# State product of an attention stage in four quadrants of TensorE, with one decay table left in PSUM and one shared bank for transposes and gate products

## The chip, the cores and the metric

The kernel runs on one core of one Trainium2 chip. Its time is the device time of one execution in microseconds (us). Six queues work side by side: PE (TensorE's matmuls; PEld is its loading of weights), DVE (VectorE), ACT (ScalarE), POOL (GpSimd), SP (SyncE, which here only issues DMAs) and the DMA engines themselves. Each engine takes its instructions in the order in which the program gives them to it, and waits for semaphores of the others.

## The reference, cut to what matters

Three stages follow one another: a recurrent attention, a mixture of 8 experts with one expert for each token, and a dense layer.

```python
for t in range(S):                       # attention, B=4, H=8, S=768, D=48
    cur = einsum('bhd,bhe->bhde', u * k[t], v[t])
    y[t] = einsum('bhd,bhde->bhe', r[t], state + cur)
    state = w[..., None] * state + einsum('bhd,bhe->bhde', k[t], v[t])
x = y as (3072, 384)
out[token] = gate * (relu(x @ w1[e]) @ w2[e])      # e = argmax of x @ w_gate
h = out @ w_in; result = (h - tanh(h)) @ w_out
```

Only the way in which the attention stage is laid out on the engines changes; all that is computed stays.

## The kernel before, in words

The attention stage is written out as a sequence of 24 blocks of 128 tokens: six chunks `c` of the sequence, and for each the four batch entries `b`; block `n` is `(c, b) = divmod(n, 4)`. The order of the work is the order in which the code of the main loop (L756 to L834) calls its helpers; no planner stands behind it. In each turn `n` of the loop the engines get:

- SP: the two loads of block n+3 (`fetch`, L239 and L240), and the store of a finished block (`xout_g`, L582), which waits for ACT. Five sets of buffers are in use.
- POOL: `side` (L342, L348) and `side_kh` (L357), products of r, k, u and a decay table for block n+2, and in `state_add` the decay of the old state (L407).
- DVE: `diag_sum` (L362), `scale` (L333: r and k of block n+1 times their decay tables), `mask` (L383: two predicated copies that put the scores under the diagonal into `am`), `state_add` (L408), and, once in four blocks, the steps of the gate (`gate`, `rank_of`, `rank_in`).
- PE: `outp` of block n-1, `state_mm` (L396) and `scores` (L378) of block n, a transpose of a finished block (`xout_t`, L573) and, once in four blocks, the gate's products (`logits` L455, `logits2` L464, `rank_mm`, `idx_mm`).
- ACT: the copies of `outp`'s results (L439), `state_copy` (L421), `xout_g` (L580), eight diagonal blocks of `am` for block n+1 (`diag`, L369), and steps of the gate.

Heads go in pairs: head h = 2j + q, and the 48 rows of q = 0 and q = 1 stand in partitions 16 to 63 and 64 to 111. `outp` adds two products in PSUM. The first (L429, from block 4 on) multiplies the state with r: its weights `Sb` are a block-diagonal copy of the state `Sc`, 112 by 128 for each pair j, so that one matmul does both heads of a pair. The second (L434) multiplies v with `am`, 128 rows by 48 columns of weights, left or right half of the array by q. The zeros of `Sb` are written once at the start (`zero_states`, L322). Every f32 matmul stands in the trace as two records. The two decay tables are made in PSUM (`PRKp`), used there for the first four blocks, and then copied to SBUF by ACT (`scale_rows`, L337).

In between, the loop prepares weights of the first expert: `w_load` (L76) loads them, and `w_split` rounds them on ACT (L84) and takes the rest on DVE (L85); the table `SPLITS` (L753) says after which block. A step of `w_split` on DVE waits for its step on ACT.

Of the kernel before, what the change touches and what calls it, by code (L numbers as in the profile page):

```python
# [15 lines left out]
ALU = mybir.AluOpType  # L16
# [14 lines left out]
def rwkv_moe_moe_kernel(ctx: ExitStack, tc: tile.TileContext, rk_t, rkv, pk, u, wp1, wp2, out):  # L31
# [168 lines left out]
    pkg = ap_.tile([P, E * HP], F32, name="pkg")  # L200
# [5 lines left out]
    Sc = [ap_.tile([PT, HP, D], F32, name=f"Sc{b}") for b in range(B)]  # L206
    Sb = [ap_.tile([PT, HP, P], F32, name=f"Sb{b}") for b in range(B)]
# [3 lines left out]
    PRK = ap_.tile([PT, 2, HP, P], F32, name="PRK")  # L211
# [36 lines left out]
    def gate_rows():  # L248
        nc.vector.memset(pkg, 0.0)
        for q in range(2):  # L250
            nc.sync.dma_start(out=pkg[64 * q:64 * q + D], in_=pk[q][:, 2 * HP:])
# [9 lines left out]
    def gate_cols():  # L261
        nc.gpsimd.memset(wgp, 0.0)
        nc.gpsimd.tensor_copy(out=wgp[:, :, 0:E], in_=pkg.rearrange("p (j e) -> p j e", e=E))
# [56 lines left out]
    def zero_states():  # L320
        for b in range(B):
            nc.scalar.mul(out=Sb[b], in_=ident[0:PT].unsqueeze(1).to_broadcast([PT, HP, P]), mul=0.0)  # L322
# [12 lines left out]
    def scale_rows():  # L335
        for k in range(2):
            nc.scalar.copy(out=PRK[:, k], in_=PRKp[k])  # L337
# [61 lines left out]
    def state_add(n):  # L399
# [3 lines left out]
        if c == 0:  # L403
            nc.vector.tensor_copy(out=Sc[b], in_=Pp[0:PT])
        else:
            sw = at2.tile([PT, HP, D], F32, tag="sw", name="sw")
            nc.gpsimd.tensor_tensor(out=sw, in0=Sc[b], in1=bc(pq[:, :, 8:9], [PT, HP, D]), op=ALU.mult)  # L407
            nc.vector.tensor_tensor(out=Sc[b], in0=sw, in1=Pp[0:PT], op=ALU.add)  # L408
        st["S", b] = n
# [1101 lines left out]
```

## Time and profile before

| | |
|---|---|
| median of 3 runs | 778.57 us (778.37 to 778.96) |
| the profiled execution, its own time | 778.02 us |
| its span, first to last instruction | 776.3 us |
| PE, PEld, DVE busy in the span | 98%, 90%, 83% |
| ACT, POOL busy in the span | 67%, 57% |
| granted clock of TensorE, mean | 0.999 |

The busy shares are averages over three stages with different limits. The attention stage fills about the first 125 us; after it PE is busy nearly all the time. Times in a timeline are counted from the start of the span. A matmul's record includes its way through the array, so records of one engine overlap, and what a group of matmuls costs is read from the start of its first record to the start of the next group. A record's own duration on DVE or ACT is likewise a little longer than the distance to the next one.

### The profile page before, as it was taken

The numbers are of one execution on the slowest core, as the hardware profiler recorded it, in microseconds if no ns is written. First come the engines' busy times: TensorE is split into PE (matmuls) and PEld (weight loads), VectorE is DVE, ScalarE is ACT, GpSimd is POOL, SyncE is SP. The second block draws the span as 40 slices with busy tenths as digits, with TensorE's granted clock in tenths as the row PEclk, the third lists the DMA queues.
The fourth block names the chain that finished last, engine by engine and source line by source line (L and its number), as shares of the span: only waits on it lengthen the run. The fifth ranks groups of instructions, "written<-read, shape, count | busy, mean of one in ns | idle before, by whom it ended". The sixth has DMA issues, their size and how long they took to land.

```text
span 776.3 us, 14324 instructions
## 1 busy us (share of the span) xinstructions
PE 762.8 (98%) x5040; PEld 695.4 (90%) x5040; DVE 645.8 (83%) x1135; ACT 523.3 (67%) x1136; POOL 440.9 (57%) x434
## 2 busy tenths in 40 slices
PE   8899999999999999999999999999999999999997
PEld 7788878998999999999889899899899899898887
DVE  7999898698898998975798888888888888888893
ACT  7999987463544554555787766776776677677881
POOL 7999972385867777766265353534435344343533
PEclk9999999999999999999999999999999999999999
DMA  8988954366899799973100010000001000000100
GB/s 253 273 258 262 288 178 145 124 192 188 245 240 297 202 291 290 251 228 104 48 1 1 1 41 1 1 21 21 1 1 41 0 1 22 21 1 0 42 1 41
DMA packets 34559, 89.63 MB, mean 115 GB/s; under 512 B 5403, under 2 KB 12608, under 8 KB 34482
## 3 DMA queue, kind: packets, MB, share of 16 engines
q1 hardware_dynamic: 30288, 78.67, 33.9%
q0 software_dynamic: 4192, 9.99, 4.2%
q8 instruction: 41, 0.67, 0.4%
q14 instruction: 36, 0.29, 0.1%
q10 hardware_dynamic: 2, 0.00, 0.0%
HBM read 72.90 MB, written 15.74 MB: 114 GB/s over the span
## 4 chain that ended last, share of the span: by engine, by line
PE 51%; issue 2%; ACT 1%; POOL 1%; POOLq 0%
PE h L1345 25%; PE o L1393 23%; PE y L1118 1%; PE hps L1093 1%; POOL out_dram L1406 0%; PE o L1345 0%; POOL g L1382 0%; POOLq L1452 0%; POOL xb L1382 0%; ACT mk L1355 0%; ACT s L1353 0%; POOLq L1506 0%; ACT xb L1381 0%; ACT z L1349 0%; ACT t L1351 0%
## 5 line engine op out<-in xcount | busy, mean ns | idle before, releaser
L1382 POOL TENSOR_TENSOR g<-t,g 128x512 fp32r<-128x512 f32 x93 | 120.4, 1295 | 176.8 <-ACT g L1381 126.7
L1345 PE MATMUL h<-xb,ring 128*128 128x512 f32 x855 | 213.6, 395 | 0.0
L1393 PE MATMUL o<-ring,g 128*128 128x384 f32 x1116 | 209.3, 336 | 0.0
L1393 PEld LDWEIGHTS o<-ring,g 128*128 128x128 f32 x1116 | 196.1, 188 | 8.2
L1345 PEld LDWEIGHTS h<-xb,ring 128*128 128x128 f32 x855 | 159.7, 188 | 30.4
L85 POOL TENSOR_TENSOR ring<-stg,ring 128x384 fp32r<-128x384 f32 x102 | 106.0, 1061 | 55.3 <-ACT ring L84 42.9
L1349 ACT ACTIVATE z<-h 128x512 f32<-128x512 f32 x95 | 56.8, 597 | 95.3 <-PE h L1345 95.3
L1118 PE MATMUL y<-h,ring 128*128 128x256 f32 (+7 forms) x576 | 114.1, 342 | 0.6 <-DVE h L1097 0.6
L1093 PE MATMUL hps<-xt,ring 128*128 128x472 f32 (+6 forms) x504 | 105.6, 353 | 0.1
L1118 PEld LDWEIGHTS y<-h,ring 128*128 128x128 f32 x576 | 101.3, 188 | 4.1 <-DVE h L1097 1.0
L1361 DVE TENSOR_TENSOR t<-t,h 128x512 f32<-128x512 f32 x95 | 65.2, 686 | 40.1 <-ACT t L1351 39.7
L1093 PEld LDWEIGHTS hps<-xt,ring 128*128 128x128 f32 x504 | 90.6, 188 | 3.7 <-DVEq L1232 0.4
L1366 DVE COPY_PREDICATED t<-mk,h 128x512 f32<-128x512 uint32 x95 | 71.5, 752 | 10.1 <-DVE h L1364 0.5
L1096 ACT ACTIVATE h<-hps 128x256 fp32r<-128x256 f32 (+7 forms) x64 | 32.0, 500 | 64.6 <-PE hps L1093 64.1
L84 ACT CAST ring<-stg 128x384 fp32r<-128x384 f32 x152 | 70.1, 513 | 7.9 <-DMA stg<-in_wp_dram 4.1
L1363 DVE SCALAR_TENSOR_TENSOR h<-s,h 128x512 f32<-128x512 f32 x95 | 66.2, 696 | 10.6 <-ACT g L1381 0.9
L1353 ACT ACTIVATE s<-z,gb 128x512 f32<-128x512 f32 x96 | 69.7, 726 | 0.0
L1355 ACT ACTIVATE mk<-z,gt 128x512 f32<-128x512 f32 x96 | 69.3, 722 | 0.0
L1364 DVE SCALAR_TENSOR_TENSOR h<-z,h 128x512 f32<-128x512 f32 x95 | 66.1, 695 | 3.3
L1362 DVE TENSOR_TENSOR h<-h,z 128x512 f32<-128x512 f32 x95 | 65.9, 693 | 0.0
L1381 ACT CAST g<-t 128x512 fp32r<-128x512 f32 x93 | 57.6, 619 | 9.7 <-DVE t L1366 7.8
L369 ACT ACTIVATE am<-ident,dt 128x128 f32<-128x128 f32 x192 | 58.6, 390 | 1.9 <-DVE dt L362 1.7
(255 smaller groups left out, 1092.3 us busy)
## 6 DMA issues: line engine op xcount, KB each, us to landing
stg<-in_wp_dram SPq DMA_DIRECT2D x64, 384.0 KB, 4.7
n<-in_rkv_dram SPq DMA_DIRECT2D x24, 576.0 KB, 5.0
d<-in_wp_dram SPq DMA_DIRECT2D x32, 384.0 KB, 5.8
t<-in_rk_t_dram SPq DMA_DIRECT2D x24, 384.0 KB, 6.9
wdec<-dcf SPq DMA_DIRECT2D x32, 192.0 KB, 5.3
xd<-xs SPq DMA_DIRECT2D x24, 192.0 KB, 2.5
stg<-wdec SPq DMA_DIRECT2D x12, 384.0 KB, 4.6
wl<-wdec SPq DMA_DIRECT2D x2, 768.0 KB, 6.2
```

Source lines behind the costliest of these rows:

```text
L84: nc.scalar.copy(out=dst[:, 0, sl], in_=of)
L85: eng.tensor_tensor(out=dst[:, 1, sl], in0=of, in1=dst[:, 0, sl].bitcast(F32), op=ALU.subtract)
L1093: nc.tensor.matmul(ps, lhsT=wf(a, kk), rhs=xt[e][b][:, kk, :], start=(n == 0), stop=(n == 8))
L1118: nc.tensor.matmul(yps[d], lhsT=wf(a)[:, d * P:(d + 1) * P], rhs=h2[:, b, :], start=(f == 0 and n == 0), stop=(f == CH1 - 1 and n == 2))
L1345: nc.tensor.matmul(ps, lhsT=wf(a, kk), rhs=xb[j][:, b, kk, :], start=(n == 0), stop=(n == 8))
L1353: nc.scalar.activation(out=s, in_=z, func=ACTF.Square, scale=G_K ** 0.5, bias=gb)
L1355: nc.scalar.activation(out=mk, in_=z, func=ACTF.Relu, scale=-1.0, bias=gt2)
L1363: nc.vector.scalar_tensor_tensor(out=ps, in0=s, scalar=G_K * G_D, in1=ps, op0=ALU.add, op1=ALU.mult)
L1364: nc.vector.scalar_tensor_tensor(out=ps, in0=z, scalar=G_A, in1=ps, op0=ALU.subtract, op1=ALU.mult)
L1366: nc.vector.copy_predicated(out=t, mask=mk.bitcast(U32), data=ps)
L1382: nc.gpsimd.tensor_tensor(out=g[:, 1, :], in0=ww, in1=g[:, 0, :].bitcast(F32), op=ALU.subtract)
L1393: nc.tensor.matmul(ops[q], lhsT=gg[i][:, b, q * P:(q + 1) * P], rhs=wf(a), start=(f == 0 and n == 0), stop=(f == CH2 - 1 and n == 2))
```

## The change

Block products are laid out anew. The state has two buffers that alternate by chunk (`Sc[0]`, `Sc[1]`), and no block-diagonal copy is made: `zero_states` and `state_copy` go. The state's product is eight matmuls instead of four, each with 64 or 48 rows and 48 columns of weights, at row half q and column half g of the array; head h = 2(2i + g) + q now lands at partitions 64g of bank `Yp[q]`. The products with `am` go in the order of q. Gate weights, the copies of `Yp` and the stores follow the new order of heads. The table for r stays in PSUM, in a bank of its own (`K`), so `scale` is two instructions of 512 elements in every block, and only the other table is copied. One bank (`X`) serves the transposes and the gate's first product; only from block 23 on they take turns with `K`. In the turns with `logits` the transpose stands behind `state_mm` instead of ahead of `outp`. `SPLITS` moves its first four steps one block ahead.

The core of the diff:

```diff
-    Sc = [ap_.tile([PT, HP, D], F32, name=f"Sc{b}") for b in range(B)]
-    Sb = [ap_.tile([PT, HP, P], F32, name=f"Sb{b}") for b in range(B)]
+    Sc = [[ap_.tile([PT, HP, D], F32, name=f"Sc{k}{b}") for b in range(B)] for k in range(2)]
...
-        if n < B:
-            for k in range(2):
-                nc.vector.tensor_tensor(out=t[:, k], in0=t[:, k], in1=PRKp[k], op=ALU.mult)
-        else:
-            nc.vector.tensor_tensor(out=t, in0=t, in1=PRK, op=ALU.mult)
+        for k, by in enumerate((PRKp[0], PRKp[1] if n < B else PRK1)):
+            nc.vector.tensor_tensor(out=t[:, k], in0=t[:, k], in1=by, op=ALU.mult)
...
-    def state_copy(n):
-        c, b = seq[n]
-        if c == C - 1:
-            return
-        for q in range(2):
-            rows = slice(64, PT) if q else slice(0, 64)
-            nc.scalar.copy(out=Sb[b][rows, :, 64 * q:64 * q + D], in_=Sc[b][rows, :, :])
...
         if c > 0:
+            for i in range(2):
+                for g in range(2):
+                    for q in range(2):
+                        rows = slice(64, PT) if q else slice(0, 64)
+                        j, p0 = 2 * i + g, 64 * g
+                        nc.tensor.matmul(Yp[q][p0:p0 + D, i, :], lhsT=Sc[c % 2][b][rows, j, :],
+                                         rhs=t_b[n % NB][rows, 0, j, :], start=(i == 0), stop=False)
+        for q in range(2):
             for j in range(HP):
-                nc.tensor.matmul(Yp[j % 2][:, j // 2, :], lhsT=Sb[b][:, j, :], rhs=t_b[n % NB][0:PT, 0, j, :],
-                                 start=(j < 2), stop=False)
-        for j in range(HP):
-            for q in range(2):
-                p0 = 64 * q
-                nc.tensor.matmul(Yp[j % 2][p0:p0 + D, j // 2, :], lhsT=n_b[n % NB][:, 2, 2 * j + q, :],
-                                 rhs=am[:, q, j, :], start=(c == 0 and j < 2), stop=(j >= 2))
+                i, p0 = j // 2, 64 * (j % 2)
+                nc.tensor.matmul(Yp[q][p0:p0 + D, i, :], lhsT=n_b[n % NB][:, 2, 2 * j + q, :],
+                                 rhs=am[:, q, j, :], start=(c == 0 and i == 0), stop=(i == 1))
...
+        turns.append(name)
+        tag = "K" if "both" in st and len(turns) % 2 else "X"
+        return ps1.tile([P, HP, P], F32, tag=tag, name=name)
...
-        SPLITS = {9: (0, 0), 13: (0, 1), 17: (0, 2), 19: (0, 3), **{NN - 3 + k: (1, k) for k in range(3)}}
+        SPLITS = {8: (0, 0), 12: (0, 1), 16: (0, 2), 18: (0, 3), **{NN - 3 + k: (1, k) for k in range(3)}}
...
-            if xs_of:
+            with_logits = n % B == 1 and n > B
+            if n == NN - 1:
+                st["both"] = True
+            if xs_of and not with_logits:
                 xout_t(xs_of[0])
```

On PE, where the state's product meets the product with `am` (here in block 10), before; yh_161 and yh_162 are the two banks `Yp`, and the first two rows stand there twice in a row:

```order
L429 MATMUL yh_161<-t_125,Sb_149 128x128
L429 MATMUL yh_162<-t_125,Sb_149 128x128
L434 MATMUL yh_161<-am,n_130 48x128 x2
L434 MATMUL yh_162<-am,n_130 48x128 x2
L434 MATMUL yh_161<-am,n_130 48x128 x2
L434 MATMUL yh_162<-am,n_130 48x128 x2
L396 MATMUL yh_163<-n_131,kh_160 64x48
```

On PE at the same place, now; the first two rows stand there four times in a row:

```order
L418 MATMUL yh_161<-t_125,Sc_145 48x128
L418 MATMUL yh_162<-t_125,Sc_145 48x128
L423 MATMUL yh_161<-am,n_130 48x128 x4
L423 MATMUL yh_162<-am,n_130 48x128 x4
L390 MATMUL yh_163<-n_131,kh_160 64x48
```

The state's matmuls are twice as many and narrower, and the four products of q = 0, which need the first masked half of `am` alone, stand ahead of the four of q = 1.

On DVE, around a step of `w_split` (L85, one of the first four) and the scaling that follows, before:

```order
L408 TENSOR_TENSOR Sc_144<-sw,yh_163 112x192
L561 TENSOR_TENSOR idf<-idf,sm 128x32
L85 TENSOR_TENSOR ring_69<-stg,ring_69 128x384
L362 TENSOR_REDUCE dt<-rku 128x8
L333 TENSOR_TENSOR t_125<-t_125,PRK 112x1024
L383 COPY_PREDICATED am<-mlt,A_1373 128x512
```

On DVE around the same step, now:

```order
L402 TENSOR_TENSOR Sc_143<-sw,yh_163 112x192
L525 SCALAR_TENSOR_TENSOR sm<-sm,RK 128x4
L527 TENSOR_TENSOR ohh<-sm,q_79 128x16
L530 TENSOR_TENSOR ol<-iotaf,sm 128x512
L85 TENSOR_TENSOR ring_69<-stg,ring_69 128x384
L356 TENSOR_REDUCE dt<-rku 128x8
L328 TENSOR_TENSOR t_129<-t_129,prkK 112x512
L328 TENSOR_TENSOR t_129<-t_129,PRK_154 112x512
L377 COPY_PREDICATED am<-mlt,A_1315 128x512
```

The step stands behind `rank_in` (three rows of the gate) one block earlier, and the one product of 1024 elements with a table in SBUF has become two of 512, of which the first reads its table (prkK) from PSUM.

On ACT, from the copies of `Yp` to the rounding of the same step (L84), before:

```order
L439 COPY y<-yh_161 128x2x128
L439 COPY y<-yh_162 128x2x128
L549 ACTIVATE rh<-hv,pid 128x4x32
L421 COPY Sb_147<-Sc_143 64x4x48
L421 COPY Sb_147<-Sc_143 48x4x48
L580 ACTIVATE xs<-Xps,gt 128x384
L369 ACTIVATE am<-ident,dt 128x128 x8
L84 CAST ring_69<-stg 128x384
```

On ACT at the same step, now:

```order
L428 COPY y<-yh_161 128x2x128
L428 COPY y<-yh_162 128x2x128
L577 ACTIVATE xs<-Xps,gt 128x384
L363 ACTIVATE am<-ident,dt 128x128 x8
L84 CAST ring_69<-stg 128x384
```

The two copies of the state are gone from every block, and the gate's row (L549) is not in this one.

## Rows read from the trace of the kernel before

**Rows 1.** Busy time by stretch: us, then each engine's busy time (instructions); later stages
```profile
core 0: us, PE busy (x) PEld busy (x) DVE busy (x) ACT busy (x) POOL busy (x), PEclk, DMA share, GB/s
130.00:365.00 235.00, 233.79 (x1388) 223.34 (x1387) 196.61 (x375) 118.45 (x267) 158.22 (x155) 1.00 0.76 220
365.00:776.00 411.00, 406.59 (x2047) 367.22 (x2045) 332.02 (x488) 290.92 (x526) 176.54 (x146) 1.00 0.04 16
```

**Rows 2.** The same view, cycles of four blocks in the attention stage
```profile
46.68:66.15 19.47, 19.17 (x280) 16.73 (x278) 18.04 (x39) 17.80 (x57) 18.86 (x20) 1.00 0.84 262
66.15:86.04 19.89, 19.44 (x280) 16.73 (x279) 18.86 (x40) 18.01 (x57) 18.49 (x19) 1.00 0.91 282
86.04:105.84 19.80, 18.76 (x265) 16.19 (x263) 17.57 (x39) 18.02 (x57) 18.33 (x18) 1.00 0.79 251
```

**Rows 3.** Waits from 20 to 106 us: us in total, times, longest us
```profile
PE yh L434 <- DVE am L383: 3.4, 7, 0.9
DVE ring L85 <- ACT ring L84: 3.3, 3, 1.4
PEld Xps L573 <- ACT xs L580: 2.5, 3, 0.8
```

**Rows 4.** Timeline of DVE: start us, us, engine line op [idle before <-releaser]
```profile
56.07 0.92 DVE L85 TENSOR_TENSOR ring<-stg,ring 128x384 fp32r<-128x384 f32 x1 [1.15 <-ACT ring L84]
...
62.26 1.22 DVE L333 TENSOR_TENSOR t<-t,PRK 112x1024 f32<-112x1024 f32 x1
63.39 1.34 DVE L383 COPY_PREDICATED am<-mlt,A 128x512 f32<-128x512 uint32 x2
```

**Rows 5.** Timeline of ACT ahead of the step of w_split in block 9
```profile
51.16 0.65 ACT L439 COPY y<-yh 128x256 f32<-128x256 f32 x2 [0.39 <-PE yh L434]
...
51.99 0.70 ACT L421 COPY Sb<-Sc 64x192 f32<-64x192 f32 x2
52.72 0.58 ACT L580 ACTIVATE xs<-Xps,gt 128x384 f32<-128x384 f32 x1
...
55.53 0.50 ACT L84 CAST ring<-stg 128x384 fp32r<-128x384 f32 x1
```

**Rows 6.** Groups by line, 20 to 106 us: count | busy us, mean ns
```profile
L85 DVE TENSOR_TENSOR ring<-stg,ring 128x384 fp32r<-128x384 f32 x3 | 3.8, 1282 | 3.3 <-ACT ring L84 3.3
```

**Rows 7.** Timeline of DVE behind the attention's loads
```profile
107.31 0.55 DVE L85 TENSOR_TENSOR ring<-stg,ring 128x384 fp32r<-128x384 f32 x1
```

**Rows 8.** Groups by line, first 230 us
```profile
L333 DVE TENSOR_TENSOR t<-t,PRK 112x1024 f32<-112x1024 f32 x20 | 32.9, 1646 | 0.0
```

**Rows 9.** Instructions of tile t on DVE: duration ns min/median/max, first and last start
```profile
L333 DVE TENSOR_TENSOR t<-t,PRK x18: 1208/1554/2496, 23.7 to 108.2; 112x1024 f32<-112x1024 f32 x18
L331 DVE TENSOR_TENSOR t<-t,prk x4: 678/680/682, 14.6 to 20.8; 112x512 f32<-112x512 f32 x4
```

**Rows 10.** Timeline of DVE and POOL at one long product of scale
```profile
32.25 2.46 DVE L333 TENSOR_TENSOR t<-t,PRK 112x1024 f32<-112x1024 f32 x1
...
32.62 1.00 POOL L342 TENSOR_TENSOR rk<-n 128x384 f32<-128x384 f32 x1
...
33.70 1.87 POOL L348 TENSOR_TENSOR rku<-rk,ub 128x384 f32<-128x384 f32 x1
```

**Rows 11.** Timeline of PE, blocks 11 and 12
```profile
63.55 1.06 PE L429 MATMUL yh<-t,Sb 112*128 112x128 f32 x8
64.53 1.22 PE L434 MATMUL yh<-am,n 128*48 128x128 f32 x15
...
66.15 1.16 PE L378 MATMUL A<-t 64*128 64x128 f32 x16
67.24 1.07 PE L455 MATMUL lps<-y,wgp 128*32 128x512 f32 x8
...
69.72 1.08 PE L434 MATMUL yh<-am,n 128*48 128x128 f32 x16
70.63 0.61 PE L396 MATMUL yh<-n,kh 128*64 128x48 f32 x16
71.17 0.60 PE L378 MATMUL A<-t 64*128 64x128 f32 x5
```

**Rows 12.** Timeline of PE in block 2
```profile
22.67 1.48 PE L434 MATMUL yh<-am,n 128*48 128x128 f32 x15 [0.92 <-DVE am L383]
23.89 0.32 PE L396 MATMUL yh<-n,kh 128*64 128x48 f32 x3
```

More of the change, by code (lines that the diff above doesn't have):

```diff
@@ L262, in gate_cols @@
         nc.gpsimd.memset(wgp, 0.0)
-        nc.gpsimd.tensor_copy(out=wgp[:, :, 0:E], in_=pkg.rearrange("p (j e) -> p j e", e=E))
+        for g in range(2):
+            rows = slice(64 * g, 64 * g + 64)
+            nc.gpsimd.tensor_copy(out=wgp[rows, :, 0:E].rearrange("p (q i) e -> p q i e", q=2),
+                                  in_=pkg[rows].rearrange("p q (i g e) -> p g q i e", g=2, e=E)[:, g])
     def in_range():
@@ L328, in scale @@
         t = t_b[n % NB][0:PT]
-        if n < B:
-            for k in range(2):
-                nc.vector.tensor_tensor(out=t[:, k], in0=t[:, k], in1=PRKp[k], op=ALU.mult)
-        else:
-            nc.vector.tensor_tensor(out=t, in0=t, in1=PRK, op=ALU.mult)
+        for k, by in enumerate((PRKp[0], PRKp[1] if n < B else PRK1)):
+            nc.vector.tensor_tensor(out=t[:, k], in0=t[:, k], in1=by, op=ALU.mult)
     def scale_rows():
-        for k in range(2):
-            nc.scalar.copy(out=PRK[:, k], in_=PRKp[k])
+        nc.scalar.copy(out=PRK1, in_=PRKp[1])
     def side_rk(n):
@@ L568, in xout_t @@
         if bank is None:
-            ps = ps1.tile([P, HP, P], F32, tag="X", name="Xps", bufs=2)
+            ps = x_bank("Xps")
         else:
@@ L672, in by_token @@
                     rT, kT = t_s[0:PT, 0], t_s[0:PT, 1]
-                    yc = ps1.tile([P, HP, P], F32, tag="X", name="yc", bufs=2)[:, 0, 0:HP]
-                    nc.vector.memset(yc, 0.0)
+                    yc = [x_bank("yc")[:, 0, 0:2] for q in range(2)]
+                    for q in range(2):
+                        nc.vector.memset(yc[q], 0.0)
                     with tc.For_i(0, P, 1) as t:
                         nc.vector.tensor_copy(out=oh, in_=bc(ident[:, bass.ds(t, 1)], [P, 64]))
-                        vb = ps1.tile([P, HP, P], F32, tag="X", name="vb", bufs=2)[:, :, 0:D]
+                        vb = sm[:, 300:300 + HP * D].rearrange("p (j d) -> p j d", d=D)
                         for q in range(2):
@@ L687, in by_token @@
                             for j in range(HP):
-                                p0, p1 = 64 * q, PT if q else 64
-                                nc.tensor.matmul(yc[p0:p0 + D, j:j + 1], lhsT=cur[p0:p1, j, :],
+                                p0, p1, o = 64 * q, PT if q else 64, 64 * (j % 2)
+                                nc.tensor.matmul(yc[q][o:o + D, j // 2:j // 2 + 1], lhsT=cur[p0:p1, j, :],
                                                  rhs=one2[p0:p1, :], start=True, stop=True)
-                        nc.vector.tensor_copy(out=st["y", c][:, :, b, bass.ds(t, 1)], in_=yc.unsqueeze(2))
-                        nc.vector.tensor_tensor(out=Sc[b], in0=Sc[b], in1=bc(wcol.unsqueeze(2), [PT, HP, D]), op=ALU.mult)
-                        nc.vector.tensor_add(out=Sc[b], in0=Sc[b], in1=kv)
+                        for q in range(2):
+                            nc.vector.tensor_copy(out=st["y", c][:, 2 * q:2 * q + 2, b, bass.ds(t, 1)], in_=yc[q].unsqueeze(2))
+                        nc.vector.tensor_tensor(out=Sc[0][b], in0=Sc[0][b], in1=bc(wcol.unsqueeze(2), [PT, HP, D]), op=ALU.mult)
+                        nc.vector.tensor_add(out=Sc[0][b], in0=Sc[0][b], in1=kv)
                 logits(c)
@@ L775, in rwkv_moe_moe_kernel @@
                 at_step(n, 6, rank_row)
-                if n > 1:
-                    state_copy(n - 1)
-            for k, m in enumerate(xs_of):
-                if k:
-                    xout_t(m)
-                xout_g(m)
+            if n > 1 and n < NN:
+                state_mm(n)
+            if xs_of and with_logits:
+                xout_t(xs_of[0])
+            if xs_of:
+                xout_g(xs_of[0])
             if 0 < n < NN - 1:
@@ L784, in rwkv_moe_moe_kernel @@
             if n < NN:
-                if n > 1:
-                    state_mm(n)
                 scores(n)
+                for m in xs_of[1:]:
+                    xout_t(m)
+                    xout_g(m)
                 mask(n)
```

40 lines of the change are left out of this document (18 added, 22 removed).

## The prediction

> **What bounds the kernel now.** I read the busy times by stretch first. From 130 us to the end PE is busy 233.8 of 235 and 406.6 of 411 us at a granted clock of 1.00, its 2.4 GHz level [rows 1]: nothing there is touched, and whatever the attention stage ends earlier, the end comes earlier too. So the question is the attention stage alone, and there I took cycles of four blocks, since the gate's steps return every fourth block. Three of them last 19.47, 19.89 and 19.80 us, and in each of them PE is busy 18.8 to 19.4, DVE 17.6 to 18.9, ACT 17.8 to 18.0 and POOL 18.3 to 18.9 us [rows 2]. Four engines are nearly full at once; to take work from one alone helps only as far as the next one.
>
> Which of them leads? A record of PE includes its way through the array, so PE looks busy through short waits: the product with `am` takes 0.91 us from its start to the next group when nothing holds it (69.72 to 70.63), and 1.22 us in block 2, where its first record has waited 0.92 us for the mask of DVE and the later ones wait for the mask's second half [rows 11, 12]. Altogether PE's named waits for that mask are 3.4 us [rows 3]. DVE's records do not overlap like that. In the three cycles it is idle 1.43, 1.03 and 2.23 us, 4.7 together, and 3.3 of these are three waits of `w_split` for ACT [rows 2, 3]. Without them DVE is full. So DVE leads, PE follows closely, and ACT enters by these three waits.
>
> **The change part by part.** The sum is made against the profiled execution, 778.02 us (span 776.3 and 1.7 around it), which lies 0.55 under the median of 778.57.
>
> *Waits of DVE for ACT.* In block 9 ACT needs 55.53 - 51.16 = 4.37 us from the copies of `Yp` to the rounding step; the two copies of the state are 52.72 - 51.99 = 0.73 of it, and a row of the gate lies in the 0.83 ahead of them [rows 5]; DVE stood 1.15 us before the step [rows 4]. Now the state's copies are gone from every block (which takes 4 x 0.73 = 2.9 us per cycle from ACT, of 17.8 to 18.0), the gate's row is not in the block to which the step has moved, and DVE has three rows of the gate ahead of it. ACT comes over 0.73 us earlier, DVE later, and ACT has 2.9 us more slack in a cycle, so I take all three waits as gone: **-3.3 us** (bounds 0 and -3.3).
>
> *The steps themselves.* Those three steps took 1282 ns on average [rows 6], one later on 0.55 us [rows 7]. The excess, 3 x 0.73 = 2.2 us, comes from POOL, as with the scaling below. Where they will meet POOL now nobody can read from this trace; I take half, **-1.1 us** (0 to -2.2).
>
> *The scaling.* Twenty products of 1024 elements take 1646 ns on average [rows 8]; to the next instruction it is about 0.09 less (62.26 to 63.39 is 1.13 for a record of 1.22 [rows 4]), so 1.56. Undisturbed it is 1.13; the mean disturbance is 0.43. The half whose table is in PSUM took 678 to 682 ns in the first blocks, hardly varying, while POOL worked [rows 9], so 0.59 to the next one; the SBUF half undisturbed is 0.57. That makes 1.16, and the question is how much of the 0.43 is left. The row to go by is the product at 32.25: it takes 2.46 us, and it ends 1.09 us after POOL's product that ran from 32.62 to 33.62, which is its own undisturbed time; POOL's next product, at 33.70, then takes 1.87 instead of 1.00 [rows 10]. That looks like one waiting for the other to finish, not like two sharing. If so, an instruction of half the length waits as long as a whole one, and each block has 1.16 + 0.43 = 1.59 against 1.56: 20 x 0.03 = **+0.6 us**. Bounds: never disturbed, 20 x -0.40 = -8.0; always as at 32.25 (1.24 more than undisturbed), 20 x (1.16 + 1.24 - 1.56) = +17. I take the mean wait, because POOL's work per cycle stays the same.
>
> The Trainium skill ("SBUF — State Buffer", section "Who interferes with whom") says the same as that row: a VectorE instruction with two inputs in SBUF and a GpSimd instruction that reads SBUF exclude each other for a whole instruction, and one with a single SBUF input is left alone. By this rule the sum is the one above; by shared bandwidth it would be 20 x (1.16 + 0.22 - 1.56) = -3.6 us, 4.2 us lower, which is one of the rivals.
>
> *The state's product on PE.* Today 8 records take 64.53 - 63.55 = 0.98 us, 0.123 each, one after another [rows 11]. It becomes 16 records, four for each quarter of the array. No row shows four quarters at work. What rows show [rows 11] is two row halves side by side (`scores`: 16 records in 67.24 - 66.15 = 1.09, 0.068 each), two column halves (16 in 0.91, 0.057 each), and four column strips: `logits`, whose 8 records of 512 elements would be 8 x 4 x 0.123 = 3.9 us one after another, is over in 1.07. Four strips ran in parallel there, so I take four quarters too: 16 x 0.123 / 4 = 0.49. The way in which the array is divided changes once more per block; `scores`, at whose borders it changes, takes 0.18 more than the 16 records of the column halves, and I take that as the price: 0.67 in all, 0.31 less per block. From PE's 18.8 to 19.4 us per cycle this leaves 17.5 to 18.2. Bounds: pairs only, 0.91 to 1.09 and 0.18, 0.1 to 0.3 more per block; no overlap, 16 x 0.123 + 0.18 = 2.15, 1.17 more. As DVE leads, a gain on PE is worth **0** by itself; what it buys is that PE does not stop the 4 us that DVE gives up.
>
> The Trainium skill ("TensorEngine Tiling (Array Packing)", section "Tiling Modes") has a rule against the change: to switch the tiling mode drains TensorE. It names no time; the 0.18 above agrees with it. Without such a price the product would cost 0.49 and the sum would stay as it is, since PE is not first.
>
> *The order of the second product.* It can start on the first masked half. In a block like block 2, where PE waits for the mask, the second half is then all that is left, and the 1.22 - 0.91 = 0.31 us go [rows 12]. Two early blocks look like this, with DVE idle for part of the block: 2 x 0.31 = **-0.6 us**. Later blocks are DVE's, and have nothing from it.
>
> *Edits I cost at nothing.* The zeroing of `Sb` and one table copy leave ACT in the first blocks, where PE's warming matmuls and the mask come last. The gate's weights take a second small copy on POOL. SP's stores wait for ACT, which hands them over 0.73 us earlier, so the loads behind them go out earlier; the first cycle moved 262 x 19.47 = 5.1 MB, and the same in 18.4 us is 277 GB/s, under the 282 of the second cycle [rows 2]. The single bank: a transpose now waits for ACT to have read the one before. ACT is done with that 0.65 + 0.58 = 1.23 us after the end of `outp`, and PE comes back to it after `state_mm` and `scores`, 0.54 + 1.09 = 1.63 us [rows 5, 11]. That leaves 0.4 us of cover; if it goes, each of some 17 transposes costs up to 0.58 us.
>
> Sum: -3.3 - 1.1 + 0.6 - 0.6 = **-4.4 us**. Against the profiled run that is 773.6, against the median 774.2; I say **774.0 us**.
>
> **The rivals.**
> 1. *DVE's disturbance shrinks* with the length of its SBUF product, or the new phase misses POOL. For it: the fastest product takes 1208 ns and half of them under 1554 [rows 9], so many meet nothing today. Against: the row at 32.25. Shared bandwidth gives 774.0 - 4.2 = 769.8, and more than half of the lower bound about 768.
> 2. *PE takes the lead back*, because the quarters overlap only in pairs or because the single bank's cover fails. Pairs put PE at 19.2 to 20 us per cycle, the bank at up to 4 x 0.58 = 2.3 over 17.5 to 18.2: both as long as today. What is left are the first blocks and little else: about 777.5.
> 3. *Slower: the quarters do not overlap at all.* Then PE needs 18.8 to 19.4 plus 4 x 1.17 = 4.7, at least 23.5 us per cycle against 19.7; in five cycles 5 x 3.8 = 19: 797. The point from which it decides is a product of about 1.3 us, where PE passes today's cycle. Against it: every division of the array that the trace shows does overlap.
> 4. *The scaling meets POOL more often*, because it now asks for SBUF at another moment. From 0.22 us more per block (4.4 over 20) the gain is gone: 778.5; from 0.3 more it is slower by what can be measured.
>
> **How the numbers follow.** The forecast 0.52, rival 1 0.20, rival 2 0.12, rival 3 0.06, rival 4 0.10. What a measurement of this kernel can tell from no change is about 0.2%, 1.6 us. The forecast's own range is 771 to 777, from its bounds other than the scaling's. The range reaches down to rival 1 (768.0) and up through rivals 2 and 4 to 778.5; it leaves out rival 3, the worse part of rival 4 and what lies beyond rival 1, together under 0.2. Faster by over 0.2% (under 777.0) are nearly all of the forecast and rival 1, and a part of 2: 0.75. Within 0.2%: the rest of 2 and half of 4: 0.15. Slower: 3 and part of 4: 0.10.
>
> **What would show it.** In the profile of the changed kernel: no wait of `w_split` on DVE for ACT in the attention stage; the PSUM half of the scaling near 0.68 us, the SBUF half between 0.66 and 1.9; the 16 records of the state's product in 0.5 to 0.7 us from start to start; cycles of four blocks near 18.5 us; DVE idle under 1 us per cycle; the transposes' wait for ACT not above today's 2.5 us. I am wrong if the state's product takes over 1 us, if the SBUF half is near its own time throughout (then the gain is larger), or if the later stages, PE's alone until now, do not start earlier by what the attention stage saves.

## The result, and the profile after

The changed kernel is faster: 771.68 us (median of 4 executions, 771.04 to 772.78) against 778.77 us beside it, a ratio of 0.9909 with a 95% interval of 0.9894 to 0.9925. Predicted were 774.0 us, with 768.0 to 778.5 as the range. Two later sets, each beside its own runs of the kernel before, gave 774.58 and 773.90 us, ratios 0.9946 (0.9928 to 0.9964) and 0.9944 (0.9920 to 0.9968). So the gain is 4 to 7 us, and its size varies from set to set; the experiments and the last section say what is known of why.

The profiled execution (772.78 us, span 771.1) answers to [rows 2] and [rows 1] as follows. Busy time by stretch: us, then each engine's busy time (instructions), granted clock, DMA share, GB/s; the first three rows are the cycles of blocks 8 to 19:

```profile
47.41:64.89 17.48, 17.48 (x312) 14.25 (x310) 17.20 (x43) 15.54 (x50) 16.09 (x18) 1.00 0.96 294
64.89:82.61 17.72, 17.57 (x312) 14.26 (x311) 17.45 (x43) 15.54 (x50) 16.31 (x18) 1.00 0.98 302
82.61:101.03 18.42, 17.38 (x297) 13.70 (x296) 18.18 (x42) 15.63 (x49) 16.27 (x18) 1.00 0.98 304
...
130.00:365.00 235.00, 233.81 (x1350) 223.40 (x1349) 191.41 (x363) 117.15 (x264) 159.30 (x155) 1.00 0.78 222
365.00:771.00 406.00, 401.33 (x2016) 361.98 (x2015) 331.42 (x487) 288.79 (x521) 174.34 (x143) 1.00 0.03 13
```

The twelve blocks took 59.16 us and take 53.62 in this trace, so 5.54 less. DVE is now idle 0.28, 0.27 and 0.24 us per cycle, where it was idle 1.43, 1.03 and 2.23 [rows 2]. The later stages are PE's as before, and carry what the attention stage saves to the end.

Groups of DVE (count | busy us, mean ns of one | idle before), the first two over the first 230 us, the third from 20 to 106 us, to be set beside [rows 6, 8]:

```profile
L328 DVE TENSOR_TENSOR t<-t,PRK 112x512 f32<-112x512 f32 x20 | 20.3, 1015 | 0.0
L328 DVE TENSOR_TENSOR t<-t,prkK 112x512 f32<-112x512 f32 x24 | 16.2, 677 | 0.0
...
L85 DVE TENSOR_TENSOR ring<-stg,ring 128x384 fp32r<-128x384 f32 x4 | 2.5, 616 | 0.0
```

The steps of `w_split` wait for nothing now (3.3 us before) and take 616 ns instead of 1282. Four of them stand in the twelve blocks now and three before, where the fourth follows at 107.31 us [rows 7]. So that is 3.3 + 3 x 1.28 - 4 x 0.62 = 4.7 of the 5.54 us. The scaling takes 0.59 + (1.015 - 0.09) = 1.52 us to the next instruction, where it took 1.56. The other two traces of the changed kernel have 985 and 958 ns for the half in SBUF, so 1.49 and 1.46 us.

The timeline of PE between blocks 11 and 12, beside [rows 11]:

```profile
62.27 0.64 PE L570 MATMUL Xps<-ident,y 128*128 128x128 f32 x4
62.84 0.66 PE L418 MATMUL yh<-t,Sc 64*48 64x128 f32 x16
63.42 1.10 PE L423 MATMUL yh<-am,n 128*48 128x128 f32 x16
64.35 0.61 PE L390 MATMUL yh<-n,kh 128*64 128x48 f32 x16
```

The state's product takes 63.42 - 62.84 = 0.58 us for 16 records, 0.98 before for 8. Four quarters of the array do work side by side.

### The profile page after: what moved, and what is told of

It reads as the page before. It is cut to its first block, busy times and chain, and to the rows that moved or that the text cites. A ratio compares the mean times of both kernels' runs of the same rounds, so it can differ in the third digit from the quotient of the medians.

```text
span 771.1 us, 14624 instructions
## 1 busy us (share of the span) xinstructions
PE 755.7 (98%) x5200; PEld 684.6 (89%) x5200; DVE 639.2 (83%) x1155; ACT 509.1 (66%) x1091; POOL 430.9 (56%) x435
## 4 chain that ended last, share of the span: by engine, by line
PE 51%; issue 2%; ACT 1%; POOL 1%; POOLq 0%
PE h L1346 25%; PE o L1394 24%; PE y L1119 1%; PE hps L1094 1%; POOL out_dram L1407 0%; PE o L1346 0%; POOL g L1383 0%; POOLq L1453 0%; POOL xb L1383 0%; ACT s L1354 0%; ACT mk L1356 0%; POOLq L1507 0%; ACT xb L1382 0%; ACT z L1350 0%; ACT t L1352 0%
## 5 line engine op out<-in xcount | busy, mean ns | idle before, releaser
L85 POOL TENSOR_TENSOR ring<-stg,ring 128x384 fp32r<-128x384 f32 x102 | 105.3, 1053 | 53.8 <-ACT ring L84 42.4
L84 ACT CAST ring<-stg 128x384 fp32r<-128x384 f32 x152 | 70.2, 512 | 9.5 <-DMA stg<-in_wp_dram 8.9
## 6 DMA issues: line engine op xcount, KB each, us to landing
wl<-wdec SPq DMA_DIRECT2D x2, 768.0 KB, 6.0
```

Source lines behind the costliest of these rows:

```text
L84: nc.scalar.copy(out=dst[:, 0, sl], in_=of)
L85: eng.tensor_tensor(out=dst[:, 1, sl], in0=of, in1=dst[:, 0, sl].bitcast(F32), op=ALU.subtract)
```

## The experiments

Three sets of four kernels; each set has its own runs of the kernel before (778.26, 778.22 and 778.38 us). "Cycles" are the three cycles of blocks 8 to 19, as above. The changed kernel itself was run beside the first and the third set only.

**The changed kernel again, as a yardstick, in two sets.**

> The changed kernel once more, unchanged, as the yardstick for the kernels beside it and for a second trace of its first 30 us. Expected by every theory: a median of 771.0 to 772.4 us (771.68 before). In the first trace the loads of v, k and r for blocks 1 and 2 landed at 9.65 and 13.62 us, against 8.84 and 11.93 us before the change, though both kernels issue them at the same times; block 3 of scores to block 4 took 5.41 us with 1.70 us of PE idle and the granted clock at 0.56 and 0.59 between 28 and 32 us. If that is chance, the loads of this trace land within 0.3 us of the times before the change at least in one of the two blocks and the clock stays at 1.00; if it belongs to the change, all of it comes back.

> The changed kernel once more, as the yardstick for the three beside it. Its medians so far were 771.7 and 774.6 us, its single runs 771.0 to 775.9, where those of the kernel before stay within 777.2 and 779.3 but for one or two. If this spread belongs to the kernel (theory: VectorE, TensorE and the loads all end close together, so small delays of a load or a fall of the granted clock reach the end), the runs here again spread over 3 us or more, around 771.5 to 774.8.

Measured: 774.58 us (771.28 to 775.89), above the 771.0 to 772.4 expected, and 773.90 us (770.11 to 777.74), as expected. The late loads came back, and so did a fall of TensorE's clock, in each of the three profiles at another place; the last section has both. The late loads of the first blocks do not matter much: with them these two traces get to block 8's scores at 45.15 and 45.52 us, the first trace at 47.41, and the kernel before, without them, at 46.68.

The three cycles add up to 57.00 and 54.73 us in these two traces, where the first trace has 53.62. In the third trace a fall of the clock lies in the last cycle (19.59 us). In the second trace the clock stays at 1.00, and the first cycle is long. Its row, and two of its waits:

```profile
45.15:66.13 20.98, 18.39 (x313) 14.72 (x311) 18.06 (x43) 15.56 (x50) 18.80 (x22) 1.00 0.99 290
```

```profile
DVE dt L356 <- POOL rku L342: 2.7, 3, 1.2
...
POOL rk L336 <- DMA n<-in_rkv_dram: 1.7, 1, 1.7
```

POOL waits 1.7 us for a load of k, r and v until 48.84 us. Behind that DVE waits 0.9 and 1.2 us for POOL (the third of its waits lies ahead), and the cycle is 3.3 us longer than the next one (17.71). Here one late load goes with the loss of more than half of the 5.54 us.

**The steps of `w_split`, in both kernels.** The edit of the changed kernel, which gets the old places; the kernel before gets the new ones by the reverse:

```diff
-        SPLITS = {8: (0, 0), 12: (0, 1), 16: (0, 2), 18: (0, 3), ...
+        SPLITS = {9: (0, 0), 13: (0, 1), 17: (0, 2), 19: (0, 3), ...
```

> The changed kernel, with the steps of w_split at blocks 9, 13, 17, 19 as before the change, and nothing else different. Over the twelve blocks 8 to 19 the change saved 5.5 us, and the three steps of w_split in them explain it by themselves: VectorE no longer waits 3.3 us for ScalarE there, and the steps take 0.55 us where they took 1.28 on average (2.0 us in all). Theory A: the 0.70 us a block of copies that ScalarE lost did this, so the casts come in time at the old places too; time within 1 us of the changed kernel (770.7 to 772.7), waits of VectorE for ScalarE at these steps below 0.8 us in all. Theory P: the place one block earlier did it; the waits of about 3.3 us come back, with the disturbance up to 5.3 us: 775.0 to 777.0 us.

> The kernel before the change, with the steps of w_split at blocks 8, 12, 16, 18 as the changed kernel has them, and nothing else different. Theory A (the freed ScalarE gave the gain): ScalarE is as full as before, the waits move with the steps: 777.8 to 779.5 us (778.8 before). Theory P (the place gave it): 773.5 to 775.5 us, with the 3.3 us of waits gone and the steps near 0.55 us.

Measured: 776.67 us (ratio 0.9980, 0.9964 to 0.9997) with the old places, so 2.1 us of the gain gone, and 775.80 us (0.9970, 0.9959 to 0.9981) for the kernel before with the new ones, a gain of 2.5. The group of the steps, 20 to 106 us, first changed kernel with old places, then kernel before with new places:

```profile
L85 DVE TENSOR_TENSOR ring<-stg,ring 128x384 fp32r<-128x384 f32 x3 | 5.1, 1693 | 1.2 <-ACT ring L84 1.2
```

```profile
L85 DVE TENSOR_TENSOR ring<-stg,ring 128x384 fp32r<-128x384 f32 x4 | 2.9, 725 | 0.7 <-ACT ring L84 0.6
```

The new place alone takes the wait from 3.3 to 0.6 us, with ACT as full as before. At the old place the freed ACT takes it to 1.2 us, but there the step meets POOL and takes 1693 ns: in block 9 it runs from 54.23 to 56.00 us, and POOL's `rk` from 54.59 to 55.58. Theory P, the place, holds, though 775.80 us lies just above its range of 773.5 to 775.5.

In the kernel before with the new steps the cycles are 19.79, 19.20 and 19.32 us, 58.31 in sum, only 0.85 under the kernel before. Yet DVE saves 3.3 - 0.6 us of waits and 3.8 - 2.9 in the steps, 3.6 us. Most of it is lost again where DVE meets POOL. Groups of DVE from 40 to 104 us, kernel before and then with the new steps:

```profile
L333 DVE TENSOR_TENSOR t<-t,PRK 112x1024 f32<-112x1024 f32 x13 | 21.2, 1628 | 0.0
```

```profile
L333 DVE TENSOR_TENSOR t<-t,PRK 112x1024 f32<-112x1024 f32 x13 | 23.2, 1788 | 0.0
...
L362 DVE TENSOR_REDUCE dt<-rku 128x8 f32<-128x384 f32 x13 | 7.1, 543 | 0.9 <-POOL rku L348 0.9
```

The scaling takes 2.0 us longer in sum, and DVE waits 0.9 us for POOL, which is busy 56.8 of the 58.3 us. PE is as full (57.0), and which of the two would stop the next saving was not tried.

**ACT's copies put back** into the changed kernel:

```diff
...
+        for q in range(2):
+            rows = slice(64, PT) if q else slice(0, 64)
+            nc.scalar.copy(out=Sb[b][rows, :, 64 * q:64 * q + D], in_=Sc[1 - c % 2][b][rows, :, :])
```

> The changed kernel, with the two ScalarE copies of the state per block put back at the place they had (into a tile that nobody reads; the products still read the state itself). Theory A (the freed ScalarE gave the gain): the copies' 0.70 us a block bring back 3.3 to 5.3 us, 775.0 to 777.0 us, ScalarE busy near 18.3 us in a cycle of four blocks that now takes 17.5 to 18.4, and VectorE waits for ScalarE at the steps of w_split again. Theory P (the earlier place of the steps gave it): within 1 us of the changed kernel, 770.7 to 772.7, with no such waits. A third, Q: the gain is neither, but the product of the state in quadrants and the scaling: also within 1 us, and then the first kernel of this set and the kernel before with new places tell P from Q.

Measured: 773.48 us (0.9942, 0.9927 to 0.9958), 1.1 less than the yardstick beside it. ACT is busy 17.82, 17.66 and 17.75 us in cycles of 18.34, 17.87 and 18.79, and the steps hardly wait, 20 to 106 us:

```profile
L85 DVE TENSOR_TENSOR ring<-stg,ring 128x384 fp32r<-128x384 f32 x4 | 2.9, 720 | 0.1
```

Theory A falls: 0.70 us a block less on ACT are worth nothing in the time.

**All but the quadrants.** The changed kernel with the block-diagonal state, its copies and the old product back, and with them the single buffer of the state and the old order of the products with `am` (of some 60 lines these):

```diff
-                        nc.tensor.matmul(Yp[q][p0:p0 + D, i, :], lhsT=Sc[c % 2][b][rows, j, :],
-                                         rhs=t_b[n % NB][rows, 0, j, :], start=(i == 0), stop=False)
+                nc.tensor.matmul(Yp[j % 2][:, j // 2, :], lhsT=Sb[b][:, j, :], rhs=t_b[n % NB][0:PT, 0, j, :],
+                                 start=(j < 2), stop=False)
```

> The changed kernel without its new state's product: a single-buffered state, the block-diagonal copy by ScalarE and its zeroing, the product of four matmuls with 112 rows, the old order of the products with the mask and the old layout of y and of the gate's weights are all back; the scaling in two halves, the single bank, the place of the transposes and the earlier steps of w_split stay as in the changed kernel. Theory Z (the prediction's: the product's 0.31 us per block on TensorE are worth 0 by themselves, since VectorE leads, and the ScalarE copies are worth nothing at the earlier steps): within 1 us of the changed kernel beside it. Theory F (TensorE follows so closely that its saving is needed): doubling the product added 0.585 us and cost some 0.3 us per block, so 0.31 us given back cost up to 0.3 in each of 20 blocks, 3 to 6 us more than the changed kernel, cycles of four blocks at 18.6 us or more with TensorE busy throughout.

Measured: 778.97 us (1.0008, 0.9994 to 1.0022), 5.1 more than the yardstick beside it: the whole gain is gone. Its cycles, and two of its waits from 20 to 106 us:

```profile
45.77:64.75 18.98, 18.80 (x281) 16.54 (x279) 17.91 (x43) 17.70 (x57) 16.17 (x20) 1.00 0.85 263
64.75:85.05 20.30, 19.19 (x282) 16.61 (x278) 19.33 (x43) 17.85 (x58) 15.62 (x19) 1.00 0.89 278
85.05:104.16 19.11, 18.80 (x266) 16.15 (x264) 17.43 (x43) 17.76 (x57) 14.54 (x17) 1.00 0.89 274
```

```profile
DVE am L379 <- PE A L374: 2.1, 6, 0.6
...
PE lps L458 <- ACT xs L583: 1.3, 4, 0.6
```

PE waits for ACT to empty the single bank, which the changed kernel's trace doesn't show. DVE no longer leads: it is idle 3.7 of the 58.4 us, where the changed kernel's first trace has 0.8 of 53.6. Groups of DVE from 40 to 104 us, this kernel and then the changed one:

```profile
L379 DVE COPY_PREDICATED am<-mlt,A 128x512 f32<-128x512 uint32 x26 | 17.7, 734 | 1.7 <-PE A L374 1.3
...
L85 DVE TENSOR_TENSOR ring<-stg,ring 128x384 fp32r<-128x384 f32 x4 | 4.0, 1001 | 0.8 <-ACT ring L84 0.7
```

```profile
L377 DVE COPY_PREDICATED am<-mlt,A 128x512 f32<-128x512 uint32 x28 | 18.8, 725 | 0.2 <-PE A L372 0.2
```

Theory F holds in the time and in the length of the cycles. By name, though, only 1.3 of the 4.8 us that the cycles lost are waits for PE's scores; 0.7 are waits for ACT at the steps of `w_split`, which also take 4.0 us again instead of 2.5. And the edit puts back more than the product: how much is due to the order of the second product or to the single state buffer was not tried. The kernel before with nothing but the new steps is faster than this one (ratio 0.9970 against 1.0008). So with the old product the split scaling, the single bank and the moved transposes together cost about 3 us.

**PE and DVE loaded on purpose.** The state's product twice, and one copy more on DVE per block:

```diff
+            for twice in range(2):
+                for i in range(2):
...
+                if n + 1 >= B:
+                    nc.vector.tensor_copy(out=spare, in_=PRKp[0][:, :, 0:D])
```

> The changed kernel, with the state's product made twice per block (the second pass starts over and overwrites the first, so the output is the same): 8 matmuls more on TensorE, at the 0.585 us that the eight take in the trace, for 20 blocks, 11.7 us of TensorE in all. The changed kernel's own time is 771.7 and 774.6 us in its two sets. Theory D (VectorE leads, TensorE waits for its masks): most of the extra time lies in waits of TensorE that are there anyway; at most 3 us more than the changed kernel, below 778. A sharper form of it, C: the granted clock fell to 1.2 GHz for some 3 us at a time in two of three profiled runs of the changed kernel, each time behind an idle stretch of TensorE, and never in those of the kernel before; with less idle it stays at 1.00, and the time is even the same or lower, 770 to 774. Rival E (TensorE leads again): 0.585 us in each block, up to 11.7 us more, 781 to 786.

> The changed kernel, with one copy of 112 x 192 numbers more on VectorE in each of 20 blocks, out of the bank of r's table into a tile that nobody reads (the state's copy of that size took 0.33 us, some 0.27 us to the next instruction). Theory D (VectorE leads): 20 x 0.27 = 5.4 us more than the changed kernel, 777 to 780. Rival E (TensorE leads): 0 to 1 us more. A third, L (the loads are the next bound, since the DMA share is 0.96 to 0.98 in the cycles): also 0 to 2 us.

Measured: 778.28 us (0.9999, 0.9984 to 1.0014) and 777.45 us (0.9990, 0.9977 to 1.0004). First cycles of each, PE's kernel first:

```profile
49.23:68.28 19.05, 19.05 (x376) 16.10 (x374) 18.00 (x42) 15.75 (x50) 15.87 (x19) 1.00 0.86 274
68.28:87.33 19.05, 19.05 (x376) 16.10 (x375) 18.00 (x43) 15.74 (x50) 15.89 (x19) 1.00 0.92 290
```

```profile
46.04:65.00 18.96, 17.85 (x313) 14.22 (x311) 18.68 (x47) 15.79 (x50) 18.19 (x22) 1.00 0.96 300
65.00:83.92 18.92, 17.82 (x312) 14.21 (x310) 18.64 (x47) 15.75 (x50) 15.86 (x19) 1.00 0.96 293
```

Against 17.6 us, PE's 4 x 0.585 = 2.3 us lengthen these cycles by 1.45 (the third by 0.8), so 0.2 us per block or somewhat more were free there. DVE's copy costs 1.2 to 1.5 us per cycle, and the estimate was 4 x 0.27 = 1.1: all of it, and a little more. DVE leads in the changed kernel, by some 0.2 us per block. In the time the doubled product costs 3.7 to 6.6 us, by the set of the changed kernel that it is held against. That is above the 3 that theory D allowed and below the 11.7 of rival E. Sharper theory C, that more work on PE would cost nothing, falls.

**The old scaling in the changed kernel:**

```diff
-        for k, by in enumerate((PRKp[0], PRKp[1] if n < B else PRK1)):
-            nc.vector.tensor_tensor(out=t[:, k], in0=t[:, k], in1=by, op=ALU.mult)
...
+        else:
+            nc.vector.tensor_tensor(out=t, in0=t, in1=PRK, op=ALU.mult)
```

> The changed kernel, with the scaling of blocks 4 to 23 as before the change: r's and k's tables both in SBUF and one instruction of 112 x 1024, nothing else different. The prediction priced the change of the scaling at 0.6 us more (0.59 + 0.57 + 0.43 against 1.56 us, with the same wait for GpSimd in the half that is left in SBUF); the trace of the changed kernel has 0.677 us for the PSUM half and 1.015 us on average for the SBUF half. Theory S (same wait, one instruction more): the old scaling is the same or up to 1 us faster than the changed kernel. Rival H (the half in PSUM escapes its share of the disturbance): the old scaling is 3 to 5 us slower, with the 1024 instruction at 1.6 us or more.

Measured: 776.72 us (0.9982, 0.9971 to 0.9993), 2.1 and 2.8 more than the two yardsticks, which were in other sets. Groups of POOL, 46 to 104 us, of this kernel and then of the changed one:

```profile
L346 POOL TENSOR_TENSOR rku<-rk,ub 128x384 f32<-128x384 f32 x12 | 19.5, 1625 | 0.9
...
L405 POOL TENSOR_TENSOR sw<-Sc,pq 112x192 f32<-112x192 f32 x12 | 8.1, 675 | 0.0
```

```profile
L342 POOL TENSOR_TENSOR rku<-rk,ub 128x384 f32<-128x384 f32 x13 | 15.2, 1171 | 1.0
...
L401 POOL TENSOR_TENSOR sw<-Sc,pq 112x192 f32<-112x192 f32 x12 | 6.1, 510 | 0.0
```

On DVE its product of 1024 takes 1685 ns, about what it took in the kernel before. The difference is on the other side: POOL's `rku` takes 0.45 us longer, and POOL is busy 56.6 of these 58 us (51.3 in the changed kernel). A fall of the clock lies in the first cycle; the two others last 18.43 and 19.47 us with POOL busy 17.99 and 18.89, where the changed kernel has 17.72 and 18.42 with 16.31 and 16.27. So of theory S and rival H neither is whole: DVE's own time hardly changes, but the split is worth 2 to 3 us. That it is worth them through POOL is read from POOL's busy time. DVE's named waits for `rku` do not prove it, since they are 3.6 us here and 1.0, 5.4 and 1.5 in the three traces of the changed kernel (20 to 106 us).

**Three ways on from the changed kernel.** The second table in PSUM too, in the free halves of the banks of `Yp`; the scaling ahead of `diag_sum`; later loads of weights:

```diff
+            for i in range(2):
+                half = t[:, 1, 2 * i:2 * i + 2]
+                nc.vector.tensor_tensor(out=half, in0=half, in1=PRKy[i], op=ALU.mult)
...
-                diag_sum(n + 1)
                 scale(n + 1)
+                diag_sum(n + 1)
...
-        LOADS = {5: (0, 0), 9: (0, 1), 13: (1, 0), 15: (1, 1), 17: (2, 0), 20: (2, 1), NN - 1: (3, 0)}
+        LOADS = {5: (0, 0), 9: (0, 1), 18: (1, 0), 20: (1, 1), 21: (2, 0), 22: (2, 1), NN - 1: (3, 0)}
```

> A version meant to go on from the changed kernel: k's table too stays in PSUM, in the unused halves of the two banks of y, so no instruction of the scaling reads two operands of SBUF. For blocks 4 to 23 the SBUF half (1.015 us) becomes two instructions of 112 x 256, estimated at 0.33 us to the next each from half of the 0.59 us of the PSUM half and a little more: about 0.27 us less per block, 5.4 us in 20 blocks. Theory D (VectorE leads): 4 to 6 us faster than the changed kernel (771.7 and 774.6 in its sets), if neither TensorE nor the loads take over. Rival L (the loads are the next bound): 0 to 2 us faster, and GpSimd's waits for the load of k, r and v grow from the 0.7 us that they have in the blocks 8 to 19. Rival B (a bank shared with the matmuls costs VectorE a wait): the two halves take over 0.5 us each and the time is the same or slower.

> A version meant to go on from the changed kernel: in each turn VectorE scales k and r of the next block before it sums rku for the diagonal, instead of after; nothing else different. VectorE's waits for GpSimd's rku were 1.0 and 5.4 us (46 to 104 us) in the two traces of the changed kernel. Theory D (these waits are on the path): scaling ahead of them fills them, 1 to 4 us faster than the changed kernel beside it. Rival M: ScalarE's eight diagonal tiles then start 1.6 us later and the mask waits for them; the same or up to 3 us slower, with waits of VectorE's mask for ScalarE in the trace. Rival S: the SBUF half of the scaling meets GpSimd at another moment, and its mean moves away from 1.03 to 1.08 us by 0.2 or more, 4 us either way.

> A version meant to go on from the changed kernel: four of the loads of the first expert's weights (0.39 MB each) go out at blocks 18, 20, 21 and 22 instead of 13, 15, 17 and 20, so 1.18 MB less move in the cycles of blocks 12 to 19, in which the DMA share is 0.98. Theory L (the loads bound these cycles): the cycles of blocks 12 and 16 get shorter, from 17.7 and 18.3 to about 17.0 and 17.3, GpSimd's waits for k, r and v vanish there, and the kernel is 1 to 2 us faster than the changed kernel beside it, with less spread. Theory D (VectorE leads, the loads only come close): the same within 0.5 us. Rival W: the later loads come too late for the steps of w_split at blocks 21 to 23, which wait for them: 1 to 4 us slower.

Measured: 879.74 us (1.130, 1.126 to 1.134), 776.96 us (0.9985, 0.9977 to 0.9994) and 773.63 us (0.9946, 0.9934 to 0.9958). No version beats the changed kernel. Timeline of PE and of DVE in the first:

```profile
119.86 1.43 PE L424 MATMUL yh<-t,Sc 64*48 64x128 f32 x16 [3.43 <-DVE t L333]
```

```profile
115.48 1.36 DVE L383 COPY_PREDICATED am<-mlt,A 128x512 f32<-128x512 uint32 x2 [5.96 <-PE A L378]
...
119.39 0.74 DVE L333 TENSOR_TENSOR t<-t,yh 112x256 f32<-112x256 f32 x2
```

The two halves take 0.74 us together, near the 2 x 0.33 expected. But PE's product into a bank waits until DVE has read the table from that bank, and the next scores stand behind it: PE and DVE take turns, a cycle takes 41 us, and the granted clock is 0.92 on average. The Trainium skill ("PSUM — Partial Sum Buffer", section "Summary: rules for kernel authors") advises to read PSUM from another bank than the one that matmuls write to, and to guard by bank with semaphores. This version keeps the guard but reads from the matmuls' own banks, and the trace shows what that costs. In the second the sums come later, and ACT's diagonal tiles wait for them:

```profile
ACT am L363 <- DVE dt L356: 20.0, 18, 2.1
```

That much was rival M, but the wait of the mask for ACT that it named is not among the waits. What DVE loses stands at the steps of `w_split`, whose casts come behind these tiles on ACT (40 to 104 us; 2.5 us and no wait in the changed kernel):

```profile
L85 DVE TENSOR_TENSOR ring<-stg,ring 128x384 fp32r<-128x384 f32 x4 | 5.2, 1288 | 1.7 <-ACT ring L84 1.7
```

In the third, the cycle of blocks 12 to 15, which lost two of the loads (251 GB/s against 302), is as long as with them, 17.72 us. The next one lost one load and got another, the one that now goes out at block 18, so the two cycles lost some 0.8 MB and not the 1.18 of the expectation:

```profile
64.44:82.16 17.72, 17.58 (x312) 14.25 (x310) 17.45 (x43) 15.54 (x50) 16.35 (x18) 1.00 0.84 251
82.16:100.59 18.43, 17.39 (x297) 13.71 (x295) 18.19 (x42) 15.63 (x49) 16.31 (x18) 1.00 0.99 311
```

In these cycles the loads do not set the pace, and theory D holds for them: a DMA share of 0.84 instead of 0.98 gains nothing. For every execution it does not hold, as the long cycle in the second trace of the changed kernel shows.

## Why the prediction was right, and where its steps were not

The time and the sign were right, and the likeliest case came true; some of the terms were right for other reasons than given.

- **Which engine leads.** DVE before PE: right, but PE is nearer than the sum needed. The sentence that the gain on PE is worth 0 by itself and keeps PE from stopping DVE's gain carries the case: everything but the quadrants (and the order and buffer that went with them) is worth nothing, and with them it is 4 to 7 us. My expectation for that run had read it as "worth nothing" (theory Z), and fell. The parts do not add up: the steps are worth 2.1 and 2.5 us, the split scaling 2 to 3 and what that run puts back 5.1, together more than the whole. The quadrants alone, without the new steps and the split scaling, were not run.
- **Waits of DVE for ACT, -3.3.** The size in the rows is right, the reason half wrong. The prediction put the freed ACT first; the runs show that the place one block earlier does most of it alone (0.6 us are left), and that the freed ACT does not show in the time.
- **The steps themselves, -1.1.** Mis-sized: 3 x (1282 - 616) ns = 2.0 us. The moved step meets POOL seldom: it takes 616, 552 and 728 ns on average in the three traces, and 0.55 us alone [rows 7].
- **The scaling, +0.6.** Wrong in sign: on DVE 1.52 against 1.56 us, 20 x -0.04 = -0.8 (down to -2.0 in the third trace), and 2 to 3 us in the time, since the old scaling put back costs that. The step that failed is "POOL's work per cycle stays the same": POOL was busy 18.86, 18.49 and 18.33 us per cycle and is now 16.09, 16.31 and 16.27. An instruction of half the length does wait about as long (0.36 us of the 0.43: 1.52 less 0.59 and 0.57), as the row at 32.25 had said, but it also holds POOL up for a shorter time (`rku` 1171 ns where the whole instruction has 1625). The waiting has two sides, and only DVE's was priced. Rival 1 (3.6 us by shared bandwidth) is near in size, but not by its mechanism.
- **The state's product, 0.67 us.** Right: 0.58, and it starts 62.84 - 62.27 = 0.57 us after the transpose ahead of it, where in the kernel before that took 108.42 - 107.93 = 0.49, so 0.66 with the switch. Rival 3 is out. The timeline of PE before:

```profile
107.93 0.66 PE L573 MATMUL Xps<-ident,y 128*128 128x128 f32 x4
108.42 1.06 PE L429 MATMUL yh<-t,Sb 112*128 112x128 f32 x8
```

- **The single bank, at nothing.** Right in the changed kernel. With the state's copies on ACT PE does wait for it: 0.7 us with the copies alone, 1.3 with the longer product as well.
- **The second product's order, -0.6.** Not seen: the first blocks differ by up to 2 us from trace to trace, and it was not run alone.
- **Loads, hidden.** Right in the first trace, by little: 294 to 304 GB/s, where the prediction had 277. In the second trace one late load makes a cycle 3.3 us longer, so in some executions they are not hidden.
- **Rival 2** was the near one: PE is 0.2 us per block behind DVE. (With pairs, 0.3 us more in each of four blocks on 19.4 us would have been 20.6 us per cycle and not 20.) That TensorE's clock could fall was not among the rivals at all, and neither was a late load.

## What to carry to other kernels

Where two engines are full together, a saving on one is worth only the distance to the other; price the pair, and test it by putting back one half of the change at a time, since here the parts, put back one by one, cost more together than the whole change had gained. When an instruction makes another engine wait, count what it costs that engine too. A step that waits may be moved to a place where its input is already there; here that did what hurrying the input did not. And where a change brings several engines and the loads close together, take more than one trace: here the same twelve blocks took 53.6, 57.0 and 54.7 us.

## What the runs showed of the hardware that was not expected

**TensorE's clock fell behind some short idle stretches of PE, and not behind others.** Busy time by stretch in the first trace of the changed kernel; PE is the second number, the granted clock the third from the end:

```profile
25.00:26.00 1.00, 1.00 (x18) 0.88 (x18) 1.00 (x3) 0.81 (x3) 0.93 (x2) 1.00 1.05 286
26.00:27.00 1.00, 0.16 (x4) 0.06 (x2) 1.00 (x2) 1.00 (x5) 0.92 (x2) 1.00 1.00 277
27.00:28.00 1.00, 0.14 (x3) 0.17 (x5) 1.00 (x3) 0.63 (x3) 1.00 (x2) 1.00 1.14 267
28.00:29.00 1.00, 1.00 (x14) 0.81 (x13) 0.93 (x6) 0.33 (x1) 1.00 (x2) 0.62 0.91 223
29.00:30.00 1.00, 1.00 (x21) 1.00 (x18) 1.00 (x6) 0.44 (x3) 1.00 (x2) 0.50 0.99 277
30.00:31.00 1.00, 1.00 (x13) 0.91 (x11) 0.87 (x2) 1.00 (x4) 0.92 (x2) 0.50 1.13 286
31.00:32.00 1.00, 1.00 (x14) 0.89 (x12) 0.00 (x0) 1.00 (x5) 1.00 (x2) 0.67 0.99 225
32.00:33.00 1.00, 1.00 (x10) 0.16 (x8) 0.81 (x2) 0.32 (x2) 1.00 (x2) 1.00 0.99 239
```

PE has waited 1.7 us for a mask, and when it works again it is at 0.50, its 1.2 GHz level, for a few us. The second trace has this behind 2.3 us of idle time at 105 us, the third from 93 us on behind 0.5 us, and the changed kernel with the old steps twice, behind 1.2 us each. There the two cycles with a fall last 20.12 and 20.10 us, the one without 19.10. The length of the stretch alone does not decide: ahead of the same product as above, at 27.4 and 27.9 us, PE stood 1.6 us in the third trace and in the kernel with ACT's copies, and the clock stayed at 1.00. The trace of the kernel before has no fall. Of 19 executions of the changed kernel 9 have a mean granted clock below 0.997, with a median of 775.78 us; the other 10 have 771.97, though one of these, the third trace at 0.997, has a fall too. Of 80 executions of the kernel before one is below. So the changed kernel pays back part of its gain in some executions; the set with 771.7 us had 1 of 4 such executions, the one with 774.6 had 4 of 6. How much of the 3.8 us is the idle time and how much the clock was not separated. Nor is it shown that the falls come because PE has less to do: below 0.997 are 3 of 24 executions of the two kernels in which PE has more work than in the changed one (the doubled product, all but the quadrants). But in the variants in which PE has as little to do as there it is anything from 1 of 11 to 7 of 12.

**Waiting in a rhythm.** How POOL disturbs the scaling's SBUF half repeats with the cycles of four blocks: from start to next the scaling takes 1.27, 1.78, 1.75 and 1.48 us in blocks 9 to 12 of the changed kernel's first trace, 1.24, 1.78, 1.75 and 1.48 in the next four, and 1.25, 1.78 and 1.76 in the three after these. The kernel with the later loads has the same rhythm, 1.25, 1.78, 1.76 and 1.49. The third trace has another one, 1.19, 1.79, 1.76 and 1.19. So a mean over blocks says little of a changed schedule.

**Left open.** The load of block 2 lets POOL start on it at 11.8 to 12.0 us in the three traced kernels that zero the block-diagonal state at the start, and at 12.4 to 14.6 in all that don't, though the loads go out at the same times. What slows them was not tried, and no run shows what it costs at the end.
